# An inverse transform on TensorE: other array tiles for its two steps, and its exchange in halves

## The chip, the cores and the metric

The kernel runs on one core of a Trainium2 chip. The metric is the device time of one execution in microseconds (us). A core has TensorE (PE, matrix multiply, into the PSUM banks), VectorE (DVE), ScalarE (ACT), GpSimd (POOL) and SyncE (SP, which here issues every DMA), each with its own instruction stream. The streams meet at semaphores.

## What is computed

The reference chains two blocks over a sequence of 2048 positions with 512 channels in bf16. Block A is a long convolution with gates, block B an MLP with shifted groups.

```python
def _A_ref(q, k, v, shift_k, ssm_k, ssm_D):
    k_shift = ...                               # 4-tap causal filter of k, per channel
    kv = k_shift * v
    L = 2 * S
    kv_f = rfft(pad(kv, S)); kf_f = rfft(pad(ssm_k, S))     # along the sequence, per channel
    y = irfft(kv_f * kf_f, L)[:S]
    return q * (y + kv * ssm_D)

def _B_ref(x, w1, w2, w3, w4):
    h = gelu(layernorm(x) @ w1)
    hs = concat(four channel groups of h, shifted by 1, -1, 2, -2 positions) @ w2
    x1 = x + hs
    return x1 + gelu(layernorm(x1) @ w3) @ w4

h = q + _A_ref(layernorm(q), k, v, ...)
out = h + _B_ref(layernorm(h), w1, w2, w3, w4)
```

(The names of the reference's wrappers are shortened here.)

## The kernel before

**The convolution** is done by transforms written as matmuls. Sequence and filter are each cut into two halves of 1024 positions (signals A0, A1 of `kv` and F0, F1 of the filter). Every signal goes through a forward transform in two steps with an exchange between them:

- `step1` (L393): matmuls of 128 rows by 32 columns, then a copy out of PSUM (a helper, L261, on ACT or DVE),
- the forward exchange (L409): DMAs on SP that move rows to other partitions, 256 KB each, eight for a signal,
- `step2` (L417): matmuls of 64 rows by 32 columns, eight tiles side by side in the array. For F1 the copy out is a fold with F0's spectrum (L429).

`conv(s, prods)` then does output half `s`: half 0 from A0*F0, half 1 from A0*F1 + A1*F0. It works in four slices `kl`. For each slice DVE multiplies the spectra (L478, two multiplications for each matmul task), and PE takes the products back through **the second step of the inverse transform** (L490, `I2`). Its sums lie in four banks of PSUM, are copied in two halves, two banks each, to a staging tile `vst` in `r_vs` (the tasks `EV`, through L261), and go by **the inverse exchange** (L500, `XI`) to `wv` in `r_z`, one DMA of 512 KB for a slice. When all four slices have landed, **the last step** (L508, `inv1`, tasks `I1`) makes four blocks of two banks, and DVE takes each bank (L624, `hsum`: gate, residual, and a sum for the layernorm).

The rest, which the prediction names: the shift filter as matmuls with diagonals (L446); 128x128 transposes (L678); `h @ w1` (L707) with its gelu (L711); `@ w2` (L730) with L733; `@ w3` (L785) with its gelu (L789); `@ w4` (L798), DVE's last sum (L800) and the store (L802). L270 is the helper for loads. `r_q`'s loads also bring the second half of the filter.

**Tables.** The factors of the transforms are built on the chip: index patterns on GpSimd, a mask with 4095, a sine on ACT. `ttab` holds the factors of the inverse's second step, `f2` those of its last step (L367, L369, L370, L380).

**Order.** Nothing is scheduled at run time. `ORDER` is a list of words such as `160S` or `158M`: a task's number, the engine that does it (`M` is ACT copying four banks at once in place of two) and the PSUM banks or buffers that it gets. `emit` walks the list and emits each task. An engine executes its instructions in that order, and a wait at the head holds back all that follows on that engine. Tasks of the convolution's second half are woven in between the MLP of the first half's blocks, so L490 and L508 stand between runs of L785, L798, L707 and L678. Buffers: eight PSUM banks, four product buffers, two staging buffers `vs`. In the instruction list a DMA also waits for the DMA issued eight before it.

Of the kernel before, what the change touches and what calls it, by code (L numbers as in the profile page):

```python
# [9 lines left out]
P = 128  # L10
# [5 lines left out]
NB = 8  # L16
# [3 lines left out]
BF16 = mybir.dt.bfloat16  # L20
# [11 lines left out]
002S 004S 003S 005S 031V 041V 042G 043G 000S 029P0 030P 059P23 001S 007S 061P45 006S 062V 067P67 010S 033V 037V 032V 069P01 008S 070V  # L32
009S 060A 068A 034V 063P23 064A 065P45 066A 023S 049G 022S 038A 035V 091P60 039V 055P23 099P71 100V 036A 044V 056A 057P45 058A 040V 101P0
102V 103P1 104V 050V 045A 347V 051A 046G 047V 105P7 106V 048A 093P2 095P3 076S 119P45 120A 094V 115P01 346V 077S 054G 024S 075S 015S
096V 097P7 078S 116A 074S 073S 092V 098V 020S 071S 350V 121P23 122A 117P45 107P01 349V 053G 108A 118V 072S 111P67 113P23 021S 114V 016S
127S 109P01 112A 110A 123S 088P4567 089V 128S 090A 085P0123 087A 082P4567 083A 348V 086V 227P21 084A 079P4501 228V 124S 080V 081A 129S 125S 131P6723
130S 134P0145 132V 133A 136A 126S 144V0 143V1 344V 147V2 146V3 135A 014S 137P2367 019S 229P4 011S 139A 018S 145P01670 153V0 152V1 138A 148P 156V2
149A 155V3 219P50 220V 150A 154P01231 157P 158M 159A 183P67 345V 336S 225P5 230V 161V0 162V1 017S 151S 226V 012S 343V 184A 140P0123 141A 231P4
142A 164V2 165V3 160S 163P67010 166P 170V0 013S 351G 167A 171V1 223P5 168A 169S 173V2 172P23671 174V3 175P 177A 195P01 224V 233P5 176V 232V 196A
178S 234V 221P6 222V 335S 352G 353G 052A 354V0 187P23 189P01 188A 185P45 186A 190V 200S 199S 191P67 192A 197P23 198V 193P01 194A 179P45 235P67  # L40
357G1 358V 363G1 359A 203S 237P23 204S 180P01 355V 360G0 356A 238V 239P45 241P23 236A 361V 378G 364V 240A 242A 206S 365A 366V0 205S 202S
201S 253S 379G 181P67 243P01 369V1 367V 372G0 244A 370V 210P2345 211V 362A 245P67 246A 371A 380G 391V 182P01 373V 027S 251S 381G0 384G1 247P23
248A 249P67 250A 368A 375G1 382P00 385P2 255S 212V 207P4567 386V 383A 387P3 254S 376V 208V 374A 216P0145 392G 393G 394A2 397A3 395P21 396A 338S
209V 404G 405G 217V 398P6 389P7 339V 388A 259P0123 377A 390A 399V 261A 256S 218V 400P6 272V0 406G 407G0 408P72 260A 410G1 402P4 417V 418G
409A 403A 411P5 412V 213P0123 401A 271V1 415P7 416A 413P5 215V 273P67230 214V 275V2 419G 420G2 423G3 421P40 414A 526P5 422A 424P0 425A 274V3 527V
528A 278V0 522P1 523V 524A 252S 277V1 428P4 276P 280V2 426P5 427A 429A 281V3 279P 282P 283A 284A 578V 579G 287V0 580G 286V1 514P0 515V
516V 262P4567 518P1 519V 521V 264A 581G0 584G1 258S 582P01 530P2 585P3 586V 520A 529V 583A 534P6 535V 263A 587P70 588A 288P01451 599P3 337S 600A
591P6 595P7 290V2 593P3 531V 289V3 592A 025S 431V 291P 292V0 293V1 295V2 296V3 026S 294P 532A 301V0 536A 635G 434V 597P2 596A 297P 594A
636G 637G 641A2 638V3 589P6 598A 533V 302V1 298A 525V 607G 608G 590A 639P72 299A 435V 257S 265P0123 267V 266A 604P6 605V 268P4501 270V 285S
305V2 304V3 642P2 643V 601P3 602V 640A 303P67010 644P20 306P 609V 645A 648P3 611A0 308V0 028S 437V 269A 649A 610V1 300S 656P2 657A 307V1 310V2  # L50
311V3 309P 317V0 312P 313A 612S 646P4 316V1 613S 319V2 654P5 318P23671 320V3 323V0 322V1 614S0 321P 314A 315S 650P0 655A 326V2 651A 652P1 606S
325V3 324P 653A 647A 430V 432V 436V 327P 328A 661P5 658P0 433V 438V 329A 330S 331P14 615P20 439G 332P36 537V 621P7 440V 444V0 441G1 442V
443A 445V 616A 447G1 448V 333P14 450G0 451V 625P2 446A 465G 466G 623P3 617P6 452V 456A1 453A0 457V 449A 454V 455A 624A 467G 478V 468V3
471V2 627P4 622A 626A 469P11 619P3 458V 490V 340G 628A 470V 618A 462V1 472P7 473A 334P24 620A 479G 480G 474P6 481A1 463V 464A 459G0 460V
461A 482G0 491G 476P7 477A 502V 484S 475A 341V 632P1 483S 542P3 492G 494V3 496S 493A2 495S 485S2 503G 504V 506G0 543V 505A1 507S 538P4
629P2 486P7 488P6 544A 539V 540A 664G 541V 487A 508S 497S0 500P3 498P4 489A 501A 342G 499A 509S1 510P7 511A 512P6 665G 666G 667V3 669S
630V 513A 554P2 668V2 555V 558P3 556A 550P4 559V 546P7 560A 692V 566P6 693G 694G 695A1 696G0 670S 671S2 672P20 603S 697S 562P3 551V 552A
678P4 679A 547V 662V 680P7 684P5 673A 674P4 548V 682P2 567V 568V 545V 675A 676P6 677A 685A 748G 698S 749G 663S 750V 751V3 752G2 699S0
570P4 563V 564V 574P3 720G 721G 575V 722G 723G1 754S 576A 633V 753S 755S1 700P60 702P5 724V0 703A 683A 726S 571V 569V 561V 572V 776V
725S 727S2 777G 517V 549V 631S 712P3 553V 565V 706P1 710P4 711A 701A 756P50 757A 708P2 709A 764P4 758P6 704P5 705A 759A 778G 780G2 782S  # L60
779V3 781S 783S0 728P20 729A 760P5 681A 738P6 739A 730P2 731A 634S 766P7 765A 761A 768P6 736P2 659V 660S 769A 732P0 737A 784P40 740P5 788P6
785A 762P2 796P4 789A 792P6 741A 794P5 763A 733A 790P2 707A 793A 797A 795A 734P0 735A 786P1 686P6 745P4 791A 742P5 767A 770P0 773P2 774V
743V 775S 771V 772S 573V 787A 713A 746V 747S 557V 577V 689P7 690V 687V 691S 801P1 802V 803S 688S 714P3 715V 716S 798P2 799V 800S
717P5 718V 744S 719S
# [32 lines left out]
def body(ctx, tc, fx, kt, q, v, sd, w1, w2, w3, w4, out):  # L97
# [50 lines left out]
    wv = {0: z1v(r_z), 1: z1v(r_z)}  # L148
# [22 lines left out]
    f2 = ct("f2", 4, 32, 4)  # L171
# [68 lines left out]
    pool.iota(n2m.rearrange("p (b q c x) -> p b q c x", b=2, q=2, c=2), pattern=[[1, 2], [16, 2], [0, 2], [2, 8]], base=0, channel_multiplier=0)  # L240
# [77 lines left out]
    kh = small("kh", 4, F32)  # L318
    mk3 = small("mk3", 4, BF16)
    s2 = early(128, BF16)  # L320
# [148 lines left out]
    def conv(s, prods):  # L469
        for kl in range(4):  # L470
# [28 lines left out]
            def f(e, sl, kl=kl, n=n):  # L499
                nc.sync.dma_start(wv[s][kl:P:4, :, :, :], vst[:, got(n, "vs")[0], :, :])  # L500
# [350 lines left out]
```

## Time and profile before

| | |
|---|---|
| time, median of 3 runs | 219.33 us (217.64 to 219.85) |
| profiled execution, first to last instruction | 215.8 us |
| mean granted TensorE clock | 0.997 |
| PE / DVE / ACT / POOL busy | 92 / 68 / 60 / 34% of the span |
| L490, second step of the inverse, matmuls 32*32 | 768, 15.9 us busy |
| L508, last step, matmuls 64*128 | 64, 8.3 us busy |
| L478, products of spectra on DVE | 48, 30.7 us busy |
| L500, inverse exchange, 512 KB | 8 issues, 3.2 / 4.6 / 5.4 us to landing (min, median, max) |

The profile is of one execution. Its time outside the span is not shown; the span is 3.5 us below the median of the runs. In lines of PE in order of time the columns are: start in us, us from the first start to the last end, line, output and inputs, array tile (rows*columns), operand, count, and in brackets the idle time ahead and what ended it. Matmuls are pipelined, so one group's end overlaps the next one's start; how long a group holds the array is read from its start to the next group's start. "SPq" is SP's instruction that issues a DMA, "PEld" the loading of weights.

### The profile page before, as it was taken

What the parts mean: (1) busy time and instruction counts of PE and PEld (TensorE: products, weight loads), DVE (VectorE), ACT (ScalarE), POOL (GpSimd) and SP (SyncE); (2) the same over time, 40 slices, a digit from 0 to 9 for tenths busy, and PEclk for the clock granted to TensorE, in tenths of its full rate; (3) what the DMA queues carried; (4) which work ended last, traced back from release to release, by engine and by line L of the source; (5) the groups of instructions that cost most, each with busy time, mean ns of one, the idle gap of its engine ahead of it and who ended that gap; (6) DMA issues with size and microseconds to landing.
All of it is one profiled execution on the core that took longest, in us unless ns stands there. A gap on an engine that the chain in (4) does not pass through costs nothing.

```text
span 215.8 us, 5937 instructions
## 1 busy us (share of the span) xinstructions
PE 199.1 (92%) x2382; PEld 116.0 (54%) x2396; DVE 147.3 (68%) x331; ACT 128.5 (60%) x210; POOL 72.6 (34%) x195
## 2 busy tenths in 40 slices
PE   7789767799879999999998999999999999999992
PEld 5254323353236646744763575565888887444440
DVE  7899999898999999789893794428787000004621
ACT  4677997789999676961960787355435757000000
POOL 7944000482786536400005586303615000000000
PEclk9999999999999999999999999999999999999998
DMA  6999799747669974020253004870564500000212
GB/s 185 378 350 310 292 352 338 239 155 266 272 232 306 389 301 146 3 100 0 65 161 100 0 2 94 153 145 25 122 148 94 127 0 3 0 0 24 97 52 73
DMA packets 29661, 32.92 MB, mean 152 GB/s; under 512 B 20417, under 2 KB 22466, under 8 KB 29378
## 3 DMA queue, kind: packets, MB, share of 16 engines
q1 hardware_dynamic: 29634, 32.54, 47.5%
q8 instruction: 19, 0.31, 0.6%
q14 instruction: 8, 0.07, 0.1%
HBM read 13.13 MB, written 4.46 MB: 81 GB/s over the span
## 4 chain that ended last, share of the span: by engine, by line
PE 72%; ACT 7%; DVE 7%; DMA 7%; issue 4%; SPq 1%; ACTq 0%; DVEq 0%
PE ps L785 23%; PE ps L798 20%; PE ps L707 7%; PE ps L490 6%; PE ps L730 6%; ACT r_a L261 4%; PE ps L446 3%; DMA r_k<-in_kt_dram 2%; PE ps L417 2%; DMA r_z<-r_vs 2%; DMA r_f<-r_a 2%; PE ps L508 2%; PE ps L678 2%; ACT r_vs L261 1%; PE ps L393 1%
## 5 line engine op out<-in xcount | busy, mean ns | idle before, releaser
L785 PEld LDWEIGHTS <-r_k 128*128 128x128 bf16 x448 | 42.9, 98 | 9.5 <-issue 3.9
L800 DVE TENSOR_TENSOR r_v<-ps,r_v 128x512 bf16<-128x512 f32 x16 | 10.7, 687 | 39.5 <-issue 31.5
L785 PE MATMUL ps<-r_dg,r_k 128*128 128x256 bf16 x280 | 32.9, 273 | 0.0
L478 DVE TENSOR_TENSOR r_p<-r_a,r_f 128x1024 bf16<-128x1024 bf16 x48 | 30.7, 685 | 2.5 <-PE ps L490 2.1
L261 ACT CAST r_a<-ps 128x1024 bf16<-128x1024 f32 x25 | 24.3, 1020 | 1.5 <-PE ps L417 0.9
L785 PE MATMUL ps<-xtx,r_k 128*128 128x256 bf16 x168 | 20.2, 273 | 0.0
L446 PE MATMUL ps<-r_dg,r_k 128*128 128x256 bf16 (+3 forms) x108 | 15.2, 285 | 4.1 <-DVE r_dg L311 2.0
L733 DVE SCALAR_TENSOR_TENSOR r_q<-r_v,hrr,ps 128x512 bf16<-128x512 bf16 x16 | 11.8, 742 | 7.9 <-PE ps L730 7.8
L490 PE MATMUL ps<-r_p,ttab 32*32 32x512 bf16 x768 | 15.9, 379 | 1.1 <-DVE r_p L478 0.5
L261 ACT CAST r_vs<-ps 128x1024 bf16<-128x1024 f32 (+1 forms) x14 | 14.5, 1075 | 3.3 <-PE ps L490 2.5
L446 PEld LDWEIGHTS <-r_k 128*128 128x128 bf16 x112 | 9.3, 98 | 12.4 <-issue 7.5
L707 PEld LDWEIGHTS <-r_fx 128*128 128x128 bf16 x128 | 11.9, 98 | 4.6 <-issue 1.7
L789 ACT ACTIVATE r_v<-ps 128x512 bf16<-128x512 f32 x14 | 8.0, 596 | 9.9 <-PE ps L785 9.9
L624 DVE SCALAR_TENSOR_TENSOR r_v<-ps,qsd,z_t 128x512 bf16<-128x512 f32 x16 | 11.4, 746 | 3.6 <-PE ps L508 3.6
L608 ACT ACTIVATE junk<-r_v 128x512 bf16<-128x512 bf16 x14 | 9.0, 641 | 8.1 <-DVE r_v L624 7.2
L756 POOL TENSOR_TENSOR xrr<-xrr,mhalf 128x2 f32<-128x2 f32 x8 | 7.0, 877 | 19.2 <-DVE xrr L753 18.9
L798 PE MATMUL ps<-w4s,r_v 128*128 128x512 bf16 x54 | 12.5, 379 | 0.1
L798 PE MATMUL ps<-w4s,r_kv 128*128 128x512 bf16 x54 | 12.5, 379 | 0.1
L707 PE MATMUL ps<-r_dg,r_fx 128*128 128x256 bf16 x96 | 11.9, 273 | 0.5 <-ACT r_dg L261 0.5
L798 PE MATMUL ps<-w4s,r_a 128*128 128x512 bf16 x55 | 12.2, 379 | 0.1
L798 PE MATMUL ps<-w4s,r_f 128*128 128x512 bf16 x55 | 12.2, 379 | 0.1
L261 ACT CAST r_f<-ps 128x1024 bf16<-128x1024 f32 x11 | 10.5, 1019 | 2.7 <-PE ps L393 2.7
(182 smaller groups left out, 350.6 us busy)
## 6 DMA issues: line engine op xcount, KB each, us to landing
r_z<-r_vs SPq DMA_DIRECT2D x8, 512.0 KB, 4.6
r_k<-in_kt_dram SPq DMA_DIRECT2D x8, 259.0 KB, 5.5
r_v<-in_v_dram SPq DMA_DIRECT2D x4, 512.0 KB, 6.1
r_q<-in_q_dram SPq DMA_DIRECT2D x8, 256.0 KB, 5.8
r_f<-r_f SPq DMA_DIRECT2D x8, 256.0 KB, 4.4
r_a<-r_a SPq DMA_DIRECT2D x8, 256.0 KB, 3.0
r_f<-r_a SPq DMA_DIRECT2D x8, 256.0 KB, 3.0
r_a<-r_z SPq DMA_DIRECT2D x8, 256.0 KB, 6.3
```

The costliest lines, as they stand in the source:

```text
L261: (act.copy if e in "AM" else on[e].tensor_copy)(o, i)
L446: nc.tensor.matmul(o[:, (d + j0) * P:(d + j1 + 1) * P], lhsT=kT[s][c][:, bb, x:x + P], rhs=diag[:, c, j0:j1 + 1, :].rearrange("p j x -> p ...
L478: on[e].tensor_tensor(out=prs[:, sl[0], :, :], in0=sp[a][:, kl, t, :, :], in1=gv, op=MUL)
L490: nc.tensor.matmul(ps[c:c + 32, bk[h], :], lhsT=ttab[32 * h:32 * h + 32, 2 * kl + t, 2 if x else xx, 32 * b0:32 * b0 + 32], rhs=prs[32 * h ...
L608: act.activation(junk[:], x, ACT.Square, accum_out=sq[:, i, 1:2])
L624: vec.scalar_tensor_tensor(out=h_sb[s][:, b, :], in0=ps[:, got(("I1", s, b // 2))[b % 2], :], scalar=qsd[:, i:i + 1], in1=z_t[:, got(("Y", ...
L707: nc.tensor.matmul(ps[:, sl[0], j * 256:(j + 1) * 256], lhsT=w1s[:, k, m * P:(m + 1) * P], rhs=xt[:, k, :], start=(k == 0), stop=(k == DC ...
L730: nc.tensor.matmul(ps[:, sl[0], :], lhsT=h1T[s][:, m, bb, x:x + P], rhs=w2s[:, m, :], start=(m == 0), stop=(m == DC - 1))
L733: vec.scalar_tensor_tensor(out=q_sb[:, s, b, :], in0=h_sb[s][:, b, :], scalar=hrr[:, 4 * s + b // 2, 0, b % 2:b % 2 + 1], in1=ps[:, got((" ...
L785: nc.tensor.matmul(ps[:, sl[0], j * 256:(j + 1) * 256], lhsT=w3s[:, k, fc * P:(fc + 1) * P], rhs=xt[:, k, :], start=(k == 0), stop=(k == D ...
L798: nc.tensor.matmul(ps[:, sl[0], :], lhsT=gb[:, fc, (b % 2) * P:(b % 2 + 1) * P], rhs=w4s[:, fc, :], start=(fc == 0), stop=(fc == FC - 1))
L800: add(("Z", s, b), {V: 0.61}, lambda e, sl, b=b: vec.tensor_tensor(out=h_sb[s][:, b, :], in0=ps[:, got(("O", s, b))[0], :], in1=h_sb[s][:, ...
```

## The change

The order of the inverse's indices is changed so that wider tiles can be used:

- **Second step:** a matmul still contracts 32 rows, but makes 64 columns where it made 32. The loop over `b0` is gone: 16 matmuls for a task where there were 32.
- **Exchange:** one DMA for each copied half of a slice, 256 KB, each with its own task right after the first one. A half writes 16 partitions (every eighth) in 8 pieces of 1024 elements, where a whole wrote 32 partitions (every fourth) in 4 pieces of 2048. A half waits for its own copy alone.
- **Last step:** a matmul contracts all 128 rows where it contracted 64; each bank takes two accumulated matmuls, where it took four. 4 matmuls for a block where there were 8.
- **Tables:** `f2` has half the columns, `ttab`'s index pattern is in another order.

`ORDER` is renumbered. On every engine the instructions come in the same order as before; each issue of the inverse exchange is two in the same place. PE's instruction list, with weight loads and matmuls counted apart, has 3962 entries where it had 4794.

```diff
-    wv = {0: z1v(r_z), 1: z1v(r_z)}
+    wv = view(r_z, 0, G, "p (k h d) -> p k h d", k=NB, h=2)
...
-    f2 = ct("f2", 4, 32, 4)
+    f2 = ct("f2", 2, 32, 4)
...
-    pool.iota(n2m.rearrange("p (b q c x) -> p b q c x", b=2, q=2, c=2), pattern=[[1, 2], [16, 2], [0, 2], [2, 8]], base=0, channel_multiplier=0)
+    pool.iota(n2m.rearrange("p (q c b) -> p q c b", q=4, c=2), pattern=[[8, 4], [0, 2], [1, 8]], base=0, channel_multiplier=0)
...
-                               ((5, 4), (6, 8), (0, 128), (1, 256), (2, 512), (3, 1024), (4, 2048)), ((5, 64), (0, 16), (1, 32), (7, 1)),
-                               ((3, -3072), (7, 3072)), ((4, 2), (2, 1)))):
+                               ((5, 4), (6, 8), (0, 128), (1, 256), (2, 512), (3, 1024), (4, 2048)), ((6, 64), (0, 16), (1, 32), (2, 8), (7, 1)),
+                               ((3, -3072), (7, 3072)), ((5, 2), (4, 1)))):
...
-    kh = small("kh", 4, F32)
+    kh = small("kh", 2, F32)
...
-    s2 = early(128, BF16)
+    s2 = early(64, BF16)
...
-    yi = ti[3][:, 0:128]
+    yi = ti[3][:, 0:64]
     def f2v(e, sl):
-        for h in range(4):
+        for h in range(2):
             on[e].tensor_scalar(out=yi[:, 32 * h:32 * h + 32], in0=n1i, scalar1=kh[:, h:h + 1], scalar2=ph3, op0=MUL, op1=ADD)
...
     add("f2", {V: 0.65, GP: 1.2}, lambda e, sl: on[e].tensor_tensor(
-        out=f2[:].rearrange("p h n q -> p (h n) q"), in0=s2.unsqueeze(2).to_broadcast([P, 128, 4]),
-        in1=mk3[:].unsqueeze(1).to_broadcast([P, 128, 4]), op=MUL), ["f2s"], port="VG")
+        out=f2[:].rearrange("p h n q -> p (h n) q"), in0=s2.unsqueeze(2).to_broadcast([P, 64, 4]),
+        in1=mk3[:].unsqueeze(1).to_broadcast([P, 64, 4]), op=MUL), ["f2s"], port="VG")
...
                             for t in range(2):
-                                for b0 in range(2):
-                                    for h in range(4):
-                                        c = 32 * (2 * b0 + t)
-                                        nc.tensor.matmul(ps[c:c + 32, bk[h], :], lhsT=ttab[32 * h:32 * h + 32, 2 * kl + t, 2 if x else xx, 32 * b0:32 * b0 + 32],
-                                                         rhs=prs[32 * h:32 * h + 32, got(("P", s, kl, i, x, t))[0], xx, :],
-                                                         start=first and xx == 0, stop=last and xx == 1)
+                                for h in range(4):
+                                    nc.tensor.matmul(ps[64 * t:64 * t + 64, bk[h], :], lhsT=ttab[32 * h:32 * h + 32, 2 * kl + t, 2 if x else xx, :],
+                                                     rhs=prs[32 * h:32 * h + 32, got(("P", s, kl, i, x, t))[0], xx, :],
+                                                     start=first and xx == 0, stop=last and xx == 1)
...
-            def f(e, sl, kl=kl, n=n):
-                nc.sync.dma_start(wv[s][kl:P:4, :, :, :], vst[:, got(n, "vs")[0], :, :])
             wd = [("X", "A1", g, k) for g in range(2) for k in range(4)] if s else []
-            add(("XI", s, kl), {SP: 0.6}, f, [("EV", s, kl, 0), ("EV", s, kl, 1)] + wd, size=620, drop=[(n, 0, "vs")])
+            for hp in range(2):
+                add(("XI", s, kl, hp), {SP: 0.6}, lambda e, sl, kl=kl, n=n, hp=hp: nc.sync.dma_start(
+                    wv[4 * hp + kl:P:8], vst[:, got(n, "vs")[0], 2 * hp:2 * hp + 2, :]), [("EV", s, kl, hp)] + wd, size=256, drop=[(n, 0, "vs")])
     def inv1(s, b):
         def f(e, sl):
-            for h in range(4):
-                for b0 in range(2):
-                    nc.tensor.matmul(ps[:, sl[b0], :], lhsT=f2[64 * b0:64 * b0 + 64, h].rearrange("p n q -> p (n q)"),
-                                     rhs=wv[s][64 * b0:64 * b0 + 64, b, h, :], start=(h == 0), stop=(h == 3))
+            for b0 in range(2):
+                for h in range(2):
+                    nc.tensor.matmul(ps[:, sl[b0], :], lhsT=f2[:, h].rearrange("p n q -> p (n q)"), rhs=wv[:, 2 * b + b0, h, :], start=(h == 0), stop=(h == 1))
         return f
```

More of the change, by code (lines that the diff above doesn't have):

```diff
@@ L36 @@
[L36 to L59, printed above, removed]
@@ L65 @@
+769A 776P6 744P2 667V 668S 777A 740P0 745A 792P40 748P5 796P6 793A 770P2 804P4 797A 800P6 749A 802P5 771A 741A 798P2 715A 801A 805A 803A 742P0 743A
+794P1 694P6 753P4 799A 750P5 775A 778P0 781P2 782V 751V 783S 779V 780S 581V 795A 721A 754V 755S 565V 585V 697P7 698V 695V 699S 809P1 810V 811S 696S
+722P3 723V 724S 806P2 807V 808S 725P5 726V 752S 727S
 """
@@ L333, in consts @@
         pool.tensor_tensor(out=tb, in0=tb, in1=n2, op=MUL)
-        pool.tensor_scalar(out=kh[:], in0=l4[:], scalar1=4.0, scalar2=k3, op0=MUL, op1=ADD)
+        pool.tensor_scalar(out=kh[:], in0=l4[:, 0:2], scalar1=4.0, scalar2=k3, op0=MUL, op1=ADD)
         pool.tensor_scalar(out=kf[:], in0=k8[:], scalar1=1.0, scalar2=kp, op0=MUL, op1=ADD)
@@ L560, in body @@
     for b in range(4):
-        add(("I1", 0, b), {PEc: 0.88}, inv1(0, b), ["f2"] + ([("I1", 0, b - 1)] if b else []) + [("XI", 0, kl) for kl in range(4)], take=[("ps", 2)], mode=4)
+        add(("I1", 0, b), {PEc: 0.88}, inv1(0, b), ["f2"] + ([("I1", 0, b - 1)] if b else []) + [("XI", 0, kl, hp) for kl in range(4) for hp in range(2)], take=[("ps", 2)])
     xall = lambda y: [("X", y, g, kl) for g in range(2) for kl in range(4)]
@@ L571, in body @@
     for b in range(4):
-        add(("I1", 1, b), {PEc: 0.88}, inv1(1, b), ([("I1", 1, b - 1)] if b else [("O", 0, x) for g in (0, 2) for x in MLP[g]]) + [("XI", 1, kl) for kl in range(4)], take=[("ps", 2)], mode=4)
+        add(("I1", 1, b), {PEc: 0.88}, inv1(1, b), ([("I1", 1, b - 1)] if b else [("O", 0, x) for g in (0, 2) for x in MLP[g]]) + [("XI", 1, kl, hp) for kl in range(4) for hp in range(2)], take=[("ps", 2)])
     allp = lambda x: [("P", 1, kl, x, k, t) for kl in range(4) for k in range(2) for t in range(2)]
```

37 lines of the change are left out of this document (28 added, 9 removed).

## The prediction, made before the changed kernel ran

> **What bounds the kernel now.** I read the list of cores first (one core, granted clock 0.997, span 215.8 us), then the chain of waits, the stretches by engine, TensorE (PE) in order of time, the DMA issues, and SP's queue.
>
> ```profile
> span 215.8 us, 5937 instructions
> ...
> PE 199.1 (92%) x2382; PEld 116.0 (54%) x2396; DVE 147.3 (68%) x331; ACT 128.5 (60%) x210; POOL 72.6 (34%) x195
> ...
> PE 72%; ACT 7%; DVE 7%; DMA 7%; issue 4%; SPq 1%; ACTq 0%; DVEq 0%
> ```
>
> PE is the bound, but not everywhere. By stretches it is busy 24.65 of the first 31 us, 12.35 of the 15 from 31 to 46 us, 12.79 of the 14 to 60 us, 14.63 of the 16 to 76 us, and 40.74 of the 41 from 76 to 117 us. Up to about 62 us VectorE (DVE), ScalarE (ACT) and the exchanges take turns with PE on the chain. From there on the chain is PE nearly without a break, and what PE saves comes off the end. The second half of the convolution lies wholly in that part:
>
> ```profile
> 107.22 1.15 PE L490 MATMUL ps<-r_p,ttab 32*32 32x512 bf16 x64
> 108.30 1.92 PE L785 MATMUL ps<-xtx,r_k 128*128 128x256 bf16 x16
> ...
> 110.15 1.13 PE L490 MATMUL ps<-r_p,ttab 32*32 32x512 bf16 x64
> 111.22 6.22 PE L798 MATMUL ps<-w4s,r_v 128*128 128x512 bf16 x27
> 118.17 1.04 PE L508 MATMUL ps<-r_z,f 64*128 64x512 bf16 x8 [0.74 <-DMA r_z<-r_vs]
> 119.14 1.05 PE L785 MATMUL ps<-r_dg,r_k 128*128 128x256 bf16 x8
> 120.12 1.04 PE L508 MATMUL ps<-r_z,f 64*128 64x512 bf16 x8
> 121.09 1.05 PE L785 MATMUL ps<-r_dg,r_k 128*128 128x256 bf16 x8
> ...
> 126.77 1.04 PE L785 MATMUL ps<-r_dg,r_k 128*128 128x256 bf16 x8
> 127.64 0.39 PE L678 MATMUL ps<-ident,nbx 128*128 128x128 bf16 x4
> 127.96 1.04 PE L508 MATMUL ps<-r_z,f 64*128 64x512 bf16 x8
> ```
>
> The reader should take three things from these starts. A block of L508 costs 0.97 us from its start to its successor's (120.12 to 121.09), though its four pairs, each two matmuls wide, stream for only 4 x 0.216 = 0.86 (0.216 is L798's pace: 14 of them in 3.02 us on the chain). The eight L785 matmuls ahead of a block of another shape take 0.98 (121.09 to 122.07), those ahead of a full-size instruction 0.87 (126.77 to 127.64). So each change between array shapes costs 0.11 us, in and out. And PE stood 0.74 us idle for the last exchange.
>
> **Second step, L490.** 768 matmuls of 32x32 become 384 of 32x64. That does not halve the time: a run of 32 takes 0.58 us up to its successor (84.56 to 85.14) and one of 64 takes 1.08, so sixteen 32x32 matmuls stream side by side in one 0.216 slot. Eight of 32x64 fill the same array, and I take the same slot. The form has no row of its own. The nearest is step two of the forward transform, L417, also eight tiles to the array (64*32):
>
> ```profile
> 96.39 0.63 PE L417 MATMUL ps<-r_a,ftab 64*32 64x512 bf16 x16
> 96.95 0.40 PE L678 MATMUL ps<-ident,nbx 128*128 128x128 bf16 x4
> ```
>
> Two slots of it take 0.56 us, 2 x 0.216 plus 0.13. So a run of one task goes from 0.58 to 0.56 (0.02 saved), and a run of two from 1.08 to 4 x 0.216 + 0.13 = 0.99 (0.09 saved, from starting fewer instructions). In the second half there are six runs of one (72.06, 75.80, 84.56, 90.80, 100.30, 101.86) and five of two. The one at 77.36 waits for VectorE's products and counts nothing, so 6 x 0.02 + 4 x 0.09 = 0.48 us. Bounds: 0 if only the slots count, 0.9 if starts cost more than I read. In the first half (31.8 to 45.3 us) the runs wait for the products of L478, and I count 0.
>
> **Last step, L508, second half.** Four blocks of eight 64-row matmuls become four 128-row matmuls for each of the four blocks: still four slots, 0.86 us, but now in the shape of the neighbours. The four blocks lose 0.97 - 0.86 = 0.11 each, 0.42. The two L785 groups ahead of blocks two and three lose 0.98 - 0.87 = 0.11 each, 0.22. The transposes ahead of block four go from 0.32 (127.64 to 127.96) to the 0.23 they take ahead of L785 (126.54 to 126.77), 0.09. Sum 0.73; bounds 0.4 and 0.9. In the first half the neighbours are L393 in 128*32, another shape either way, so the changes of shape stay and I count 0. One gain there and here is left out of the sum: the first bank is complete after two slots, not four, so DVE's L624 can start 0.43 us earlier; after 118 us DVE is not the bound.
>
> **The exchange, L500.** Eight issues of 512 KB become sixteen of 256 KB.
>
> ```profile
> r_z<-r_vs SPq DMA_DIRECT2D x8, 512.0 KB, 4.6
> ...
> r_f<-r_f SPq DMA_DIRECT2D x8, 256.0 KB, 4.4
> r_a<-r_a SPq DMA_DIRECT2D x8, 256.0 KB, 3.0
> ```
>
> Above, the issues with KB each and median us to landing; below, the chain ahead of the second half's last step.
>
> ```profile
> 112.24 1.03 ACT r_vs L261
> 113.26 0.02 issue
> 113.28 4.84 DMA r_z<-r_vs
> ```
>
> ACT copies the two halves of the last slice one after the other (two copies of 0.97 us from 111.33). Today the transfer waits for both and lands at 118.12. Then the first half can go at 112.3, and the second at 113.28 with half the bytes. With the 3.0 us of the other 256 KB exchanges the second lands at 116.3, with 4.4 at 117.7. PE can use it from 117.27 (28 matmuls of L798, of which one has no record, from 111.22 at 0.216). I take the lower row, as nothing else is moving there (the slice of the page from 113.3 to 118.7 us has 100 GB/s, which is 540 KB, that one transfer; SP issues nothing else between 108.8 and 129.5 us). Then the wait goes whole: 118.17 - 117.27 = 0.90 us, one change of shape with it. Bounds: 0.9 and 0.05, the latter if the second half lands with the whole of today. Next late is PE's own work. The pieces shrink from 4 KB to 2 KB; in this trace the transfers in 2 KB pieces (the loads of r_q, 256 KB) land in 5.8 us beside much traffic, so the price is unclear there too, and is held by these bounds.
>
> The Trainium skill, page "DMA: Bandwidth & Descriptors", section Rules for kernel authors, speaks against the split: two transfers to disjoint partition halves serialize, and one should be used. No row here shows two such halves. By it the wait would shrink by half a microsecond and not vanish (first rival).
>
> **SP's queue.** An issue of L500 takes 0.536 to 0.586 us, so four more in each half are 2.2 us of SP. Behind the first half's stand the load of the second weights (47.19) and the exchange of F1 (L409, first at 50.64, released by ACT). SP is idle from 47.74 to 50.64, 2.9 us, and in the instruction lists of both kernels each DMA also waits for the one eight before it, which here will be halves issued at least 5 us earlier. Cost 0; without that cover up to 2.2 us, as L409 is on the chain at 52.47. In the second half SP waits for ACT before L500 33.1 us in all, so 0 too. The two loads of r_q between the first exchanges start 0.6 us later, 4 us before L393 reads them at 47.55.
>
> **Tables.** On GpSimd L367 falls from four to two (1.75 to 0.87 us) and L380 halves (1.32 to 0.7), with one more memset (0.04). GpSimd is done with them at 19.2 us and the first L490 runs at 31.8; DVE's L361 at 16.47 comes after a BN_STATS, not after GpSimd. Cost and gain 0.
>
> **Sum.** 0.48 + 0.73 + 0.90 = 2.11 us off a span of 215.8, so 213.7. The median of the runs shown, 219.33, is 3.5 above that span (they go from 217.64 to 219.85, and no view shows what lies outside it). I keep the 3.5: **217.2 us**. One per cent, about what a measurement of this kernel can tell from no change, is 2.2 us, so the forecast lies on that edge.
>
> **Rivals.**
> 1. *The wait at 118 us stays in part.* For: the other 256 KB exchanges reach 4.4 and 6.3 us. If the halves run one behind the other, they end 4.84 + 0.56 after 112.3, at 117.7, and save 0.47 in place of 0.90: 217.6. If the second half lands as the whole does today, the sum is 1.2 to 1.3: 218.1. Against: bytes are halved where the queue is empty. Chance 0.16.
> 2. *The early part gains too.* PE makes 832 of its 4794 instruction issues fewer, and so fewer fetches (the queue named "instruction": 19 packets, 0.31 MB). One issue of L409 near 53 us took 1.85 us where the median is 0.59, and PE waited 0.64 us for what it sent. If that, and PE's waits of 0.2 to 0.5 us from 60.9 to 63.5 us, ease, 0.6 us or more comes on top: 216.6 or less. Against: ACT, full from 46 to 60 us (13.68 of 14), sets that stretch. Chance 0.22.
> 3. *Slower: 32x64 tiles do not run eight abreast.* No row shows the form. If its weight loads or streams let four through at a time, a slot pair costs 0.43 more per task: 16 tasks in the bound half, 6.9 us, and up to 3.4 in the first: 219.3 - 1.6 + 6.9 = 224.6 or more. It decides from a slot of 0.27 us (1.63 us over 32 slots is 0.05). Against: the L490 weight loads already overlap, 64 of 87 ns each within 0.84 us. The Trainium skill, page "TensorE: Matmul & The Clock Gate", section LDWEIGHTS, lets a load take time with its columns, 53 ns for 64, and eight in a row would be 0.43; sixteen loads of 32 would be as much, and the trace shows 0.216, so they overlap. Chance 0.09.
> 4. *The first half slips:* SP's extra issues reach the exchange of F1, 2.2 us given back, 219.4. Chance 0.05.
>
> **How the numbers follow.** The forecast has 0.48, half of it on each side of the 1% edge. Faster: 0.24 + 0.22 = 0.46. Same: 0.24 + 0.16 + 0.05 = 0.45. Slower: 0.09. The range leaves out the third rival and the far end of the second: down to 215.4 (upper bounds of the terms, 0.9 + 0.9 + 0.9, and 1.85 - 0.59 of early gain), up to 219.9 (the fourth rival, with the 0.5 us that the runs spread above their median).
>
> **What would show it.** Right: L490 in two-task runs near 0.99 us and one-task runs near 0.56; L508's successor blocks 0.86 us after their start and L785 ahead of them at 0.87; no PE idle time against r_z at about 117 us, the last half landing under 4 us after its issue. Wrong: L490 groups longer than 0.27 us a slot; SP late at the exchange of F1; a new PE wait after 118 us in place of the old.

## The result, and the profile after

| | before | after |
|---|---|---|
| time, median (lowest to highest), 11 runs each | 217.97 us (217.39 to 219.85) | 216.65 us (216.0 to 217.74) |
| ratio after / before, 95% interval | | 0.9917 (0.989 to 0.9944) |
| profiled execution | 215.8 us | 214.2 us |
| 16 KB fetches on the queue named "instruction" | 19 | 15 |

The change makes the kernel faster by 0.8%, 1.8 us by the ratio and 1.3 us by the medians; the two profiled executions differ by 1.6 us. Here and below, medians and ratios leave out runs more than 1.5% above the fastest of their kernel. The page of the kernel after gives the span, the busy time of PE, the chain's shares and the inverse exchange (issues, KB each, median us to landing):

```profile
span 214.2 us, 5136 instructions
...
PE 198.7 (93%) x1980; PEld 114.8 (54%) x1980; DVE 147.9 (69%) x331; ACT 128.3 (60%) x210; POOL 72.3 (34%) x194
...
PE 73%; ACT 9%; DMA 7%; issue 4%; DVE 3%; SPq 3%; DVEq 0%; ACTq 0%
...
r_z<-r_vs SPq DMA_DIRECT2D x16, 256.0 KB, 3.5
```

The bound is PE as before. In the kernel after, the lines have moved: the second step is L486 (L490 before), the last step L504 (L508), the product with w3 L780 (L785), w4 L793 (L798), w1 L702 (L707), the transposes L673 (L678), the inverse exchange L497 (L500), the copy helper L259 (L261). The kernels with unused matmuls further down are two lines on (L488, L506, L782, L795, L704). PE in order of time:

```profile
106.34 1.07 PE L486 MATMUL ps<-r_p,ttab 32*64 32x512 bf16 x32
107.34 1.92 PE L780 MATMUL ps<-xtx,r_k 128*128 128x256 bf16 x16
109.19 1.07 PE L486 MATMUL ps<-r_p,ttab 32*64 32x512 bf16 x32
110.19 6.22 PE L793 MATMUL ps<-w4s,r_v 128*128 128x512 bf16 x28
116.25 1.03 PE L504 MATMUL ps<-r_z,f 128*128 128x512 bf16 x4
117.11 1.04 PE L780 MATMUL ps<-r_dg,r_k 128*128 128x256 bf16 x8
117.99 1.03 PE L504 MATMUL ps<-r_z,f 128*128 128x512 bf16 x4
...
125.18 0.39 PE L673 MATMUL ps<-ident,nbx 128*128 128x128 bf16 x4
125.40 1.03 PE L504 MATMUL ps<-r_z,f 128*128 128x512 bf16 x4
126.26 1.91 PE L702 MATMUL ps<-r_dg,r_fx 128*128 128x256 bf16 x16
...
135.78 1.91 PE L702 MATMUL ps<-xtx,r_fx 128*128 128x256 bf16 x16
138.90 3.34 PE L702 MATMUL ps<-r_dg,r_fx 128*128 128x256 bf16 x29 [1.21 <-DMA r_dg<-dhb]
```

Three things are to be read from it. The last step starts at 116.25, straight after the 28 matmuls ahead of it: the idle time of 0.74 us in front of it is gone. A block of it holds PE 0.86 us (116.25 to 117.11) and the eight matmuls behind it 0.88 or 0.87, so the changes of shape are gone there. But at 138.90 stands an idle time of 1.21 us that the kernel before does not have, for a DMA that brings transposed rows (`r_dg<-dhb`). There the same two groups follow each other without a gap, though only just: the rows land at 140.23, and PE, after sixteen matmuls in 1.75 us, is ready for them at 140.21.

```profile
138.46 1.91 PE L707 MATMUL ps<-xtx,r_fx 128*128 128x256 bf16 x16
140.28 3.77 PE L707 MATMUL ps<-r_dg,r_fx 128*128 128x256 bf16 x32
```

Set beside the same instructions of before, the lead is 0.77 us at the second half's first run of the second step (71.29 for 72.06), 1.03 at 110.19 (111.22), 1.92 at the last step's first block (118.17), 2.67 at 126.26 (128.93). The new wait takes 1.2 us of it back, and 1.5 to 1.6 reach the end. So the questions are three: what made the wait at 118 us go, what made the wait at 138.9 us come, and what the two steps are worth without them.

A hint is in the records of single transfers in the traces. A DMA here is done in 16 parts, each of which has its own landing. In both waits 15 parts had landed in time and one was late, beside a 16 KB transfer on the "instruction" queue. I take these to be the fetches of PE's next instructions: there are 19 for 4794 entries in PE's list and 15 for 3962, one for about 256.

```
kernel, transfer (us)           issue    15 parts   last part   fetch: start, took
before, r_z whole               113.28   116.61     118.12      115.82, 0.95
after, r_z first half           111.36   114.40     114.45      116.79 (after both)
after, r_z second half          112.27   115.56     115.57
after, r_dg (at 138.9 us)       134.11   137.29     138.85      136.55, 1.12
```

Before, PE was ready for the exchange at 117.27, 0.66 us after 15 of 16 parts were there. With 832 instructions fewer in PE's list, the fetches fall elsewhere: one missed the exchange and another hit `r_dg`. **Theory:** the place of the fetches made one wait go and the other come, and the halves have no part in it. **Rival:** the halves freed PE at 118 us, and the wait at 138.9 us is what is next late on the chain, whatever the fetches do.

### The profile page after: what moved, and what is told of

Its sections match the earlier page's. It is cut to its first block, busy times and chain, and to the rows that moved or that the text cites. A ratio compares the mean times of both kernels' runs of the same rounds, so it can differ in the third digit from the quotient of the medians.

```text
span 214.2 us, 5136 instructions
## 1 busy us (share of the span) xinstructions
PE 198.7 (93%) x1980; PEld 114.8 (54%) x1980; DVE 147.9 (69%) x331; ACT 128.3 (60%) x210; POOL 72.3 (34%) x194
## 4 chain that ended last, share of the span: by engine, by line
PE 73%; ACT 9%; DMA 7%; issue 4%; DVE 3%; SPq 3%; DVEq 0%; ACTq 0%
PE ps L780 23%; PE ps L793 21%; PE ps L725 6%; PE ps L702 6%; PE ps L486 6%; ACT r_a L259 3%; PE ps L444 3%; DMA r_dg<-dhb 2%; PE ps L504 2%; DMA r_fx<-in_fx_dram 2%; PE ps L415 2%; ACT r_z L259 2%; PE ps L391 2%; ACT junk L603 2%; DMA r_z<-r_vs 2%
## 5 line engine op out<-in xcount | busy, mean ns | idle before, releaser
L780 PEld LDWEIGHTS <-r_k 128*128 128x128 bf16 x448 | 43.2, 98 | 9.4 <-issue 3.2
L795 DVE TENSOR_TENSOR r_v<-ps,r_v 128x512 bf16<-128x512 f32 x16 | 10.7, 687 | 39.4 <-issue 31.4
L780 PE MATMUL ps<-r_dg,r_k 128*128 128x256 bf16 x280 | 32.9, 273 | 0.0
L259 ACT CAST r_a<-ps 128x1024 bf16<-128x1024 f32 x25 | 24.2, 1021 | 1.2 <-PE ps L391 0.6
L780 PE MATMUL ps<-xtx,r_k 128*128 128x256 bf16 x168 | 20.2, 273 | 0.0
L444 PE MATMUL ps<-r_dg,r_k 128*128 128x256 bf16 (+3 forms) x112 | 16.0, 288 | 2.1 <-ACT r_f L259 1.7
L486 PE MATMUL ps<-r_p,ttab 32*64 32x512 bf16 x384 | 15.6, 383 | 1.2 <-DVE r_p L476 0.5
L259 ACT CAST r_vs<-ps 128x1024 bf16<-128x1024 f32 (+1 forms) x14 | 14.5, 1075 | 3.2 <-PE ps L486 2.3
L702 PEld LDWEIGHTS <-r_fx 128*128 128x128 bf16 x128 | 12.2, 98 | 5.4 <-issue 1.5
L784 ACT ACTIVATE r_v<-ps 128x512 bf16<-128x512 f32 x14 | 8.0, 596 | 9.7 <-PE ps L780 9.6
L702 PE MATMUL ps<-r_dg,r_fx 128*128 128x256 bf16 x96 | 11.8, 273 | 1.7 <-DMA r_dg<-dhb 1.2
L793 PE MATMUL ps<-w4s,r_kv 128*128 128x512 bf16 x56 | 12.7, 379 | 0.0
L793 PE MATMUL ps<-w4s,r_v 128*128 128x512 bf16 x56 | 12.6, 379 | 0.0
L793 PE MATMUL ps<-w4s,r_a 128*128 128x512 bf16 x56 | 12.2, 379 | 0.0
L793 PE MATMUL ps<-w4s,r_f 128*128 128x512 bf16 x56 | 12.2, 379 | 0.0
L391 PEld LDWEIGHTS <-f 128*32 128x32 bf16 x256 | 5.6, 96 | 11.7 <-issue 7.0
```

The source lines that it names most:

```text
L259: (act.copy if e in "AM" else on[e].tensor_copy)(o, i)
L444: nc.tensor.matmul(o[:, (d + j0) * P:(d + j1 + 1) * P], lhsT=kT[s][c][:, bb, x:x + P], rhs=diag[:, c, j0:j1 + 1, :].rearrange("p j x -> p ...
L486: nc.tensor.matmul(ps[64 * t:64 * t + 64, bk[h], :], lhsT=ttab[32 * h:32 * h + 32, 2 * kl + t, 2 if x else xx, :], rhs=prs[32 * h:32 * h + ...
L702: nc.tensor.matmul(ps[:, sl[0], j * 256:(j + 1) * 256], lhsT=w1s[:, k, m * P:(m + 1) * P], rhs=xt[:, k, :], start=(k == 0), stop=(k == DC ...
L780: nc.tensor.matmul(ps[:, sl[0], j * 256:(j + 1) * 256], lhsT=w3s[:, k, fc * P:(fc + 1) * P], rhs=xt[:, k, :], start=(k == 0), stop=(k == D ...
L793: nc.tensor.matmul(ps[:, sl[0], :], lhsT=gb[:, fc, (b % 2) * P:(b % 2 + 1) * P], rhs=w4s[:, fc, :], start=(fc == 0), stop=(fc == FC - 1))
```

## The experiments

There are eleven runs, in three jobs, each beside the kernel before on the same chip. Where a time is compared, it is by its ratio to that, or by the medians of one job.

### The kernel after again, and with 39 unused matmuls

The first has no edit. The second puts matmuls whose result nobody reads ahead of A0's second step, where PE idles at 25 to 31 us, so that everything behind them moves in the list of instructions:

```diff
     def step2(sig, kl):
         def f(e, sl):
+            for _ in range((11, 14, 14, 0)[kl] if sig == "A0" else 0):
+                nc.tensor.matmul(ps[:, sl[0], 0:P], lhsT=wup, rhs=wup, start=True, stop=True)
```

> The changed kernel once more, as the measure for the other three. If the 1.2 us wait of the product with w1 (L702) for the transposed rows r_dg comes from a fetch of PE's instructions that stands at a fixed place of the program (about PE's 3000th recorded instruction), the wait is there again at 138 to 139 us, 0.8 to 1.5 us long, with one of the sixteen parts of that transfer late. If it was chance in one execution, it is gone here, and the span is about 213.

> 39 unused matmuls (78 instructions with their weight loads) are added in the early waits for the exchange of A0 (27 to 31 us). Nothing is left out. Theory (instruction fetches delay one part of a transfer): the fetch now near 136.6 us moves to about 129, the one near 116.8 to about 110, no transfer that PE waits for is hit, the wait for r_dg at 138 us falls from 1.2 to under 0.2 us, and the kernel is 0.8 to 1.3 us faster than the changed kernel. Rival (the transposes through memory now start too late for PE, which reaches them 2.7 us sooner): the wait stays 1.0 us or more, and the time is the changed kernel's or up to 0.3 us above it.

Measured: 0.9905 (0.9864 to 0.9945) for the kernel after again, and 0.9875 (0.9818 to 0.9932) with the unused matmuls, 215.87 us. The first has the wait for `r_dg` again, 1.27 us at 141.23, and a fetch at 138.75 beside it (15 parts at 139.62, the last at 141.19). The second, PE in order of time:

```profile
111.86 6.22 PE L795 MATMUL ps<-w4s,r_v 128*128 128x512 bf16 x28
117.91 1.03 PE L506 MATMUL ps<-r_z,f 128*128 128x512 bf16 x4
...
137.44 1.91 PE L704 MATMUL ps<-xtx,r_fx 128*128 128x256 bf16 x16
139.19 3.66 PE L704 MATMUL ps<-r_dg,r_fx 128*128 128x256 bf16 x32
```

The group that read `r_dg` at 138.90 with a gap follows here without one (137.44 + 1.75 = 139.19). The fetches are now at 112.66 and 128.80, and the 16 parts of `r_dg`, issued at 135.80, land within 0.15 us of each other, at 138.88 to 139.03, 0.16 us ahead of PE. So the wait at 138.9 us is the fetch's, though without it the rows come only just in time. The time is 0.47 us below the kernel after again (216.34), where 0.8 to 1.3 was expected, and the intervals overlap: that the wait goes is read from the trace, not from the time.

### The kernel before with the same 39 unused matmuls

The same two lines, put into the kernel before.

> The kernel before with the same 39 unused matmuls. The fetch near 115.8 us, beside the last inverse exchange, moves to about 111. Theory (the whole 512 KB exchange was late only because that fetch held back one of its sixteen parts): it lands 3.2 to 3.6 us after its issue where it took 4.84, PE's wait of 0.74 us for r_z at 118 us is gone, and the kernel is 0.6 to 1.0 us faster than before, without any halves. Rival (a whole exchange can't land sooner; the halves gave the 0.9 us): landing stays above 4.5 us, the wait stays, the time is that of before within 0.3 us.

Measured: 0.9919 (0.9889 to 0.9949), 216.83 us. That is as much as the whole change gave, with no part of the change in it. Its PE in order of time (lines two on from before: L510 is the last step, L787 the product with w3, L709 that with w1), and its exchange:

```profile
111.25 6.22 PE L800 MATMUL ps<-w4s,r_v 128*128 128x512 bf16 x28
117.40 1.04 PE L510 MATMUL ps<-r_z,f 64*128 64x512 bf16 x8
118.37 1.05 PE L787 MATMUL ps<-r_dg,r_k 128*128 128x256 bf16 x8
...
137.68 1.91 PE L709 MATMUL ps<-xtx,r_fx 128*128 128x256 bf16 x16
139.43 3.66 PE L709 MATMUL ps<-r_dg,r_fx 128*128 128x256 bf16 x32
```

```profile
r_z<-r_vs SPq DMA_DIRECT2D x8, 512.0 KB, 3.5
```

The whole 512 KB, issued at 113.31, has landed at 116.66, 3.35 us later (15 parts at 116.57), with the fetch at 111.76 for 0.96 us, over before the issue. Neither wait is there. Up to the product with w4 this execution and that of before stand within 0.03 us of each other (111.25 and 111.22), and the last step starts 0.77 us sooner (117.40 for 118.17): that much is the wait alone. The median to landing of the eight is 3.5 us where before had 4.6. The rival falls: a slice need not be halved for PE to be freed at 118 us.

The Trainium skill, page "DMA: Bandwidth & Descriptors", section Rules for kernel authors, says that two transfers to disjoint partition halves serialize. The runs agree in that nothing is won: a second half, issued 0.9 us behind the first, takes 3.30 us from issue to landing (112.27 to 115.57) and with the unused matmuls 3.31, where the whole takes 3.35. The next run, where the two are issued 0.6 us apart, shows the second held up.

### The last exchange's two issues in the other order

In `ORDER` the two words of the last slice's halves are swapped (`337S 338S` to `338S 337S`), so that the first half is issued behind the second, when both copies are done.

> The changed kernel with the two issues of the last inverse exchange in the other order, so that both wait for the second copy. Nothing is left out. Theory (the early start of the first half is not what freed PE): the last half lands 0.5 to 0.7 us later than now, at about 115.9 to 116.3 us, and PE, ready at 116.25, waits 0.1 us at most; time as the changed kernel within 0.3 us. Rival (the early start is the gain): PE waits 0.6 us or more for r_z, and 0.6 to 0.9 us are given back.

Measured: 0.9924 (0.9888 to 0.996), 216.77 us. SP's queue and PE:

```profile
114.23 1.17 SPq L497 DMA_DIRECT2D r_z<-r_vs  x2
```

```profile
112.16 6.22 PE L793 MATMUL ps<-w4s,r_v 128*128 128x512 bf16 x28
118.48 1.02 PE L504 MATMUL ps<-r_z,f 128*128 128x512 bf16 x4
```

28 matmuls at 0.216 end at 118.21, and the step starts at 118.48: a wait of 0.27 us. The theory had 0.1 us at most and the rival 0.6 or more, so the early start is worth something, but little. The halves were issued at 114.23 and 114.82 and landed at 117.33 and 118.35, after 3.10 and 3.53 us, the pair 4.1 us after its first issue. A whole, issued at 114.23, would be there at 117.58 by the 3.35 us above. So a pair of halves is slower than a whole by the second issue and more, and the early start of the first half only makes up for that. In the time 0.27 us can't be seen (216.77 for 216.34 us, the intervals overlap). The wait for `r_dg` is there as in the kernel after, 1.27 us.

### Each step undone alone

The kernel after with its 39 unused matmuls is the control, repeated in this job. One kernel takes the last step back to 64 rows for a matmul, one takes the second step back to 32 columns:

```diff
-            for b0 in range(2):
-                for h in range(2):
-                    nc.tensor.matmul(ps[:, sl[b0], :], lhsT=f2[:, h].rearrange("p n q -> p (n q)"), rhs=wv[:, 2 * b + b0, h, :], start=(h == 0), stop=(h == 1))
+            for j in range(4):
+                for b0 in range(2):
+                    h, r = j // 2, 64 * b0
+                    nc.tensor.matmul(ps[:, sl[b0], :], lhsT=f2[r:r + 64, h].rearrange("p n q -> p (n q)"), rhs=wv[r:r + 64, 2 * b + b0, h, :],
+                                     start=(j == 0), stop=(j == 3))
```

```diff
-                                for h in range(4):
-                                    nc.tensor.matmul(ps[64 * t:64 * t + 64, bk[h], :], lhsT=ttab[32 * h:32 * h + 32, 2 * kl + t, 2 if x else xx, :],
+                                for b0 in range(2):
+                                    for h in range(4):
+                                        c = 64 * t + 32 * b0
+                                        nc.tensor.matmul(ps[c:c + 32, bk[h], :], lhsT=ttab[32 * h:32 * h + 32, 2 * kl + t, 2 if x else xx, 32 * b0:32 * b0 + 32],
...
```

> The kernel after with the 39 unused matmuls, unchanged from the run before, as the control for the three beside it. Expected: ratio 0.987 to 0.990 to the kernel before, no wait of the second group of the first product with w1 for the block's rows near 138 us, the last step's first block right after the fourth product near 118 us.

> The last step alone goes back to eight matmuls of 64 rows for a block; each bank takes its own 64 rows twice, so half of each sum is left out of the result and another half is in it twice. Second step, halves of the exchange and unused matmuls stay. Theory (the shape of the array costs about 0.11 us at each change, in and out, and the last step's gain in the bound stretch is that): blocks of the last step cost 0.97 us again in place of 0.86, the groups of eight of the product with w3 ahead of them 0.98 in place of 0.87, and the time is 0.6 to 0.9 us above the control. Rival (the gain of the change is in the second step, and the last step's is taken back by a later wait): same blocks, but less than 0.3 us above the control.

> The second step alone goes back to 32 columns for a matmul, twice as many of them for a task, with the tables, the halves of the exchange, the last step and the unused matmuls of the control; nothing is left out. Theory (a wider tile saves no slot, only starts and fetches): one-task runs 0.58 and two-task runs 1.08 us up to their successors in place of 0.57 and 1.00, four two-task runs in the bound stretch, so 0.2 to 0.5 us above the control, if no fetch of PE's instructions falls on a transfer that PE waits for. There are 384 matmuls more, so more fetches, and they shift: if one falls between 113 and 117 us or between 134 and 139 us, a wait of 0.7 to 1.3 us comes back at the last exchange or at the second group of the product with w1. Rival (half the matmuls is half the time): 6 us or more above the control.

Measured: control 0.9867 (0.9836 to 0.9897), 215.66 us. Last step at 64 rows 0.9909 (0.9877 to 0.994), 216.71: 1.05 us above the control by the medians, 0.92 by the ratios. Second step at 32 columns 0.9887 (0.9849 to 0.9925), 216.48: 0.82 us above it by the medians, 0.44 by the ratios. In none does PE wait for a DMA of `r_z` or `r_dg` behind 100 us. First the kernel with 64 rows (L507 is the last step, L784 the product with w3), then the one with 32 columns (L490 is the second step), PE in order of time:

```profile
117.68 1.04 PE L507 MATMUL ps<-r_z,f 64*128 64x512 bf16 x8
118.65 1.05 PE L784 MATMUL ps<-r_dg,r_k 128*128 128x256 bf16 x8
119.63 1.04 PE L507 MATMUL ps<-r_z,f 64*128 64x512 bf16 x8
```

```profile
104.85 1.15 PE L490 MATMUL ps<-r_p,ttab 32*32 32x512 bf16 x64
105.93 1.92 PE L784 MATMUL ps<-xtx,r_k 128*128 128x256 bf16 x16
107.78 1.15 PE L490 MATMUL ps<-r_p,ttab 32*32 32x512 bf16 x64
```

A block of 64 rows holds PE 0.97 us again and the group behind it 0.98; over the stretch from the first block to the end of the fourth the control is 0.74 us shorter. A two-task run of 32 columns holds PE 1.08, of 64 columns 1.00 (106.34 to 107.34 above); from the run at 72 us to the last step's first block the control is 0.32 us shorter (44.96 for 45.28 us). The rest of the differences in the times, 0.1 to 0.5 us, is less than the intervals (about 0.7 us each way), and so is the whole of the second step's: what that step is worth rests on the trace.

### Filling the idle time at 57 to 63 us

The profile of the kernel after that ran again shows something else. Columns: stretch, length, busy time of the engines (instructions), then the granted clock of PE, the DMA share and GB/s.

```profile
57.00:64.00 7.00, 5.23 (x70) 2.24 (x71) 6.86 (x19) 7.00 (x15) 5.75 (x16) 1.00 0.57 208
64.00:67.40 3.40, 3.40 (x33) 1.88 (x32) 3.04 (x6) 2.15 (x5) 2.84 (x10) 0.51 0.99 323
67.40:90.00 22.60, 22.60 (x272) 13.74 (x270) 21.54 (x49) 17.52 (x33) 10.74 (x22) 1.00 0.67 241
```

The clock is at half for 3.4 us behind a stretch in which PE idled 1.77 of 7 us, and in the same execution at half from 30 to 33.3 us too. To the control, 20 more unused matmuls were added in that stretch: 12 ahead of the first transposes and 8 ahead of the first product with w1.

> The control with 20 further unused matmuls in the stretch where PE idles between 57 and 63 us: 12 ahead of the first transposes and 8 ahead of the first product with w1. Theory (a stretch with much idle time brings the granted clock to half for 3.4 us afterwards, in some executions): no half clock at 63 to 67 us, the time 0 to 1 us below the control and less spread. Rival (the half clock comes by something other than idle time, or the unused matmuls delay the work behind them): the half clock is still there in the profile, or the time is 0.5 us or more above the control. The fetches of PE's instructions move by 20 matmuls too, so the waits near 118 and 138 us are to be looked at again before the time is read.

Measured: 0.9864 (0.9838 to 0.989), 215.82 us (215.22 to 215.99), against the control's 215.66 (215.26 to 216.5). Half clock there is none, but the control's profile has none in this job either, so the run does not tell whether the added work keeps the clock up. In time it can't be told from the control.

### 14, 18 and 22 unused matmuls

To put the fetch on the halves of the exchange themselves.

> The kernel after with 14 unused matmuls in the place of the 39. With none, the 16 KB fetch of PE's instructions starts at 116.8 us, after the last exchange, and with 39 at 111.4 to 112.7, before its data move; 14 should bring it to about 114.9 us, 2 to 3 us after the issue of the second half, where the kernel before had it (2.5 us after). Theory (the fetch makes the last part late, halves or not): the second half's last part lands 0.8 us or more after its 15th, and if that is later than PE's fourth product with w4 ends, PE waits up to 1 us at the last step. Rival (halves of 256 KB in 2 KB pieces keep the fetch from mattering): the last part within 0.2 us of the 15th although the fetch lies inside the transfer. If the fetch misses the window, the run says nothing.

> The same with 18 unused matmuls: the fetch at about 114.3 us, 2 us after the issue of the second half. Theory and rival as with 14: the last part 0.8 us or more after the 15th, against within 0.2 us.

> The same with 22 unused matmuls: the fetch at about 113.8 us, between the data of the first half and those of the second. Theory and rival as with 14; here either half can be the late one.

Measured, one run each beside one of before at 217.95 us: 217.35, 216.7 and 218.07 us, of which the first and third have the half clock once (means 0.992 and 0.989). In the first two the fetch missed the exchange: it started at 118.47 and 117.48 us, after both halves had landed. In the third it started at 114.55, 0.25 us ahead of the second half's issue. No part of that half is late (the last 0.06 us behind the 15th), but SP's issue of it takes 1.20 us where it takes 0.53 in the kernel after, and it lands at 118.47, 0.31 us before PE comes to it. So on these two halves no late part was seen. An earlier slice shows it, in the kernel after itself: 15 parts of the half issued at 93.25 land by 96.24 and the last at 97.08, beside a fetch at 94.61. In the run with 22 a half issued at 94.31 has its last part 1.50 us behind the 15th. So halves are held up as a whole is, and the rival of these runs falls; PE did not wait for those two. And the three runs hit something else. In the run with 18, SP's queue and PE; below them SP's queue with 39:

```profile
131.17 1.04 SPq L668 DMA_DIRECT2D dhb<-nbx  x2
132.37 2.18 SPq L670 DMA_TRANSPOSE xtx<-dhb  x1
134.65 1.08 SPq L668 DMA_DIRECT2D dhb<-r_k  x2
135.89 2.76 SPq L670 DMA_TRANSPOSE r_dg<-dhb  x2
```

```profile
136.63 1.91 PE L704 MATMUL ps<-xtx,r_fx 128*128 128x256 bf16 x16
139.60 3.67 PE L704 MATMUL ps<-r_dg,r_fx 128*128 128x256 bf16 x32 [1.07 <-DMA r_dg<-dhb]
```

```profile
131.98 1.12 SPq L668 DMA_DIRECT2D dhb<-nbx  x2
133.27 1.18 SPq L670 DMA_TRANSPOSE xtx<-dhb  x1
134.55 1.08 SPq L668 DMA_DIRECT2D dhb<-r_k  x2
```

The wait for `r_dg` is back, 1.07 us, although its own 16 parts land within 0.45 us (139.11 to 139.56). Here the fetch, at 132.03 for 1.39 us, lay on the write to `dhb` at 131.17: 15 parts at 133.19, the last at 134.62. The transpose issued next held SP 2.18 us where it holds it 1.18 with 39, and all that follows on SP was issued 1 us later. It does not need that write: by its semaphores, the writes that it waits for are the pair before, landed by 130.42, and it ends at 134.55, ahead of the late part. So the issue itself took longer beside the fetch, as that of the half above did; why is not shown. With 14 and 22 the same place is hit (last parts 1.1 and 1.5 us behind the 15th, transposes of 1.81 and 2.16 us), and PE waits 0.33 and 0.38. So a fetch need not fall on the transfer that PE waits for; one during an issue ahead of it on SP does as well.

## Why the prediction was right or wrong

The forecast of 217.2 us is 0.55 above the measured 216.65, well inside its range, and the change was to be worth 2.1 us and is worth 1.3 to 1.8. Part of the agreement is luck: the median of before was taken from three runs at 219.33 and is 217.97 over eleven, and a term that was missing in the sum (0.77 us gained early) and one that was missing on the other side (the new wait, 1.2) cancel in part. From 217.97 the same sum would have given 215.9, 0.8 below the measured time.

**Last step, 0.73 us: right.** Blocks of 0.86 us and neighbours of 0.87 came as read from the changes of shape; in the trace it is 0.75, and 0.74 when undone alone.

**Second step, 0.48 us: the mechanism right, the size too large.** Eight 32x64 tiles do run in one slot, and half the matmuls is far from half the time. One-task runs take 0.570 us (predicted 0.56, before 0.583) and two-task runs 1.002 (0.99, before 1.08). What came is 0.26 us in the trace, and 0.32 when undone alone. Two runs of the second half gave nothing but took: the run at 76.56, which waits for DVE's products and was counted at nothing, got 0.09 us longer, and the one-task run at 89.98 takes 0.66 where it took 0.61. So what was too large is the term "6 x 0.02 + 4 x 0.09 = 0.48 us": four of the two-task runs gain 0.08 each, five of the one-task runs 0.01, and the two just named lose.

**The exchange, 0.90 us: the size right, the reason wrong.** PE is no longer idle there, 0.89 us. But the step "then the first half can go at 112.3, and the second at 113.28 with half the bytes" is not why. Half the bytes saved 0.05 us of landing (3.30 for 3.35), and the whole slice is in time when no fetch lies on it. What the prediction took for the length of the transfer, 4.84 us, was one part of 16, held up beside a fetch. The profile of before could have shown it: the same 512 KB landed in 3.2 us at the least, and 15 of the 16 parts of this one in 3.33. The 540 KB that the prediction read as "that one transfer" are the transfer, 524 352 bytes, and one fetch of 16 384.

**"Next late is PE's own work": wrong.** Next late was a transfer at 138.9 us, by 1.21 us, again by a fetch. The prediction named "a new PE wait after 118 us in place of the old" as what would show it wrong, and that is what came; it had no price in the sum. The fewer fetches stood in the second rival, as a gain alone and for the early part alone.

**Tables and SP's queue, 0: not contradicted.** SP's first issue of the exchange of F1 is 1.1 us earlier than before (49.53 for 50.64), the lead that PE has there. The fourth rival did not happen.

**The early part, 0: wrong, in part as the second rival had it.** After is 0.77 us ahead at 71.3 us. In before, the exchange of F1 was hit by a fetch too (52.67 us, 1.85 us long; one issue's last part 2.3 us behind its 15th), and PE waited 0.64 us for it, which the prediction saw without its cause; after has no such wait, though a fetch met its exchange as well (52.54 us, 0.93 us long; last part 1.33 us late). That is not all of the 0.77, and the executions with 39 unused matmuls and full clock up to there reach the same run anywhere between 71.69 and 72.62 us. What else moves the early part stays open.

**The first rival**, that the halves serialize and the wait stays in part, was right in part on the transfers (issued 0.6 us apart, the second takes 3.53 us where the first takes 3.10) and wrong on the wait, since the length was not what made PE wait. **The third rival** did not happen: a two-task run of 1.00 us is 4 x 0.216 and 0.13, as read from the forward transform's tiles.

What the two steps are worth by themselves, with no fetch on either wait, is the control against the kernel before with the same unused matmuls: ratios of 0.9867 and 0.9875 against 0.9919, about 1.0 us. By the medians of the one job that has both it is 215.87 against 216.83 us, and no run of the one reaches the other's. Their terms in the trace give 0.74 + 0.32. The profiled execution of the change as it stands gained about that, 0.9 from a fetch that went away and 0.8 in the early part, and lost 1.2 to a fetch that came.

One thing more was not settled. The kernel before gains 1.8 us by the ratio from its 39 unused matmuls, where the two profiles show 1.0. Part of the rest goes with the clock (below): among runs with a mean clock above 0.992 the gain is 1.5 us (218.15 over ten runs, 216.69 over eight). What the other half of a microsecond is stays open.

## What to carry to other kernels

Before a transfer's length is put down to its size, look at when its parts landed: if 15 of 16 are in time, the size is not what makes it late, and a smaller transfer is not the cure. A change that alters the number of instructions moves every later fetch of them, so a wait that goes or comes far from the change should be tried against the old kernel with a few unused instructions before it is credited to the change. And tiles of another shape pay at the borders with their neighbours: 128 rows in place of 64 gained nothing in the slots, and all of its 0.74 us in the changes of shape.

## What was not expected of the hardware

**Fetches of PE's instructions delay transfers.** A 16 KB fetch takes 0.9 to 1.9 us, and one part of a transfer that it meets can land 1 us and more behind the other 15 (1.4 to 1.6 for those issued at 113.28, 134.11 and 131.17 above). It does not always: of the 668 transfers issued after 78 us in the thirteen profiles, 158 had such a fetch between their issue and their 15th part, and 68 of these had the last part over 0.5 us late. Of the 510 without one, 6 had. The edits move the fetch and the late part together; how a fetch holds a part up is not shown. The Trainium skill, page "Runtime: NRT & Kernel Launch", section Instruction fetch mechanics, has the blocks of 16 KiB and 256 instructions, and the trace agrees; it calls the cost mostly hidden, and here it is 1.2 us where a transfer on the path is hit.

**The clock drops in some executions.** It goes to half for 3.4 us, seven times in the thirteen profiles, drops at the very end of a span not counted. In the 3.4 us ahead of each, PE was idle for 38 to 59% of the time, in pieces of 1.9 us at the longest. That is not enough by itself: the kernel after idles 58% of such a stretch (26.6 to 30 us) and keeps its clock. In the first job 15 of 25 runs of before had a mean clock of 0.992 or less (one such drop takes 0.008 off the mean), with a median of 219.28 us, where the ten others had 218.15. Of the kernels with 39 or more unused matmuls, 3 of 34 runs had such a mean. Whether the added matmuls bring that about is argued and not shown.
